# Landmark sums of two batches: strided sums on VectorE, or products with the identity on TensorE

## The chip, the cores and the metric

The kernel runs on one core of a Trainium2 chip. The metric is the device time of one execution in microseconds (us), as a median over runs. The engines are TensorE (PE, its weight loads PEld), VectorE (DVE), ScalarE (ACT), GpSimd (POOL) and SyncE (SP), whose queue issues most of the DMAs.

## What is computed

Three stages follow each other: attention by landmarks, a dense layer with squared ReLU, and a layer of eight experts of which each token uses one. Only the first matters here; its beginning is the sum over segments:

```python
batch, n_heads, seq, head_dim = (8, 8, 576, 64); m = 32; scale = 1.0 / np.sqrt(D)
q_lm = q.reshape(B, H, m, S // m, D).mean(axis=3)      # 32 landmarks, each the mean of 18 rows
k_lm = k.reshape(B, H, m, S // m, D).mean(axis=3)
A = sm(q, k_lm); Bm = sm(q_lm, k_lm); C = sm(q_lm, k)  # softmax of scaled scores
# Z: an iterated inverse of Bm, 6 steps
attn = A @ Z @ C @ v
h = np.maximum(x @ w_in, 0.0); x = (h * h) @ w_out     # x: attn, (4608, 512)
# then gate, argmax over 8 experts, that expert's two layers
```

Everything is fp32, up to the argmax.

## The kernel before

A batch's attention is a *unit*, written as a Python generator: the sums of keys and queries, transposes, landmarks, scores, softmax, the seven steps of the inverse, and a matrix `wt` by which `w_in` becomes G for this batch. The dense layer of a batch, `gemm`, takes G and the transposed A (`at`) and runs two column halves times 16 steps of `hp` (six products, L998), ReLU and square (ScalarE and VectorE, L1009 to L1012) and `acc` (twelve products, L1045). It is the main loop.

Batch 0's unit runs alone at first, in `prologue`, at a high priority, beside the conversion of the weights `w_in` and `w_out` (`convert`: two ScalarE operations, L153 and L154, two of VectorE, L163 and L164, one of GpSimd, L167, for each piece; `w_out` is split into two parts besides). Then come the first parts of G (`first_g_of`, L827, L834, L837), and `gemm(0)`, into which the unit of batch 1 is woven by a rate, and so on for each next batch. The program is traced once; a planner then lays down each engine's order by priority and readiness in its own model of the times. On the chip every engine takes its instructions in that fixed order.

A tile `t` holds the keys or the queries of four heads: 128 partitions (head, landmark) by 18 rows by 64 columns, loaded by one DMA of 576 KB from SP's queue. Keys and queries share three such buffers (one more for the last of batch 0). The next load is issued by `load_next` when a tile's transposes are done.

Batches 0 and 1 (`u["pe"]`, b below `PE_BATCHES`) turn keys and queries over by transposes on TensorE (`transposed`, L395, three to a bank, recorded under the helper's line L349, then a ScalarE copy L398). For the later batches VectorE does it.

The sums (`sums`) are the same for all batches: two strided VectorE reductions over the 18 rows (L382), and a GpSimd copy (L385) that puts the 64 columns a second time beside the first, since the scores need the landmarks in both halves of the partitions. `landmarks` transposes the sums of both head groups (two transposes) and copies the result out on ScalarE (L447). Products of the unit run through `matmul` and stand under L346.

PSUM banks come from `self.banks`: seven in the prologue, three in the first G, and from then on the three of `aux` alone, which the unit, G and the routing share.

Of the kernel before, what the change touches and what calls it, by code (L numbers as in the profile page):

```python
# [9 lines left out]
F32 = mybir.dt.float32  # L10
# [4 lines left out]
ALU = mybir.AluOpType  # L15
# [4 lines left out]
B, H, S, D = 8, 8, 576, 64  # L20
# [63 lines left out]
class Kernel:  # L84
# [214 lines left out]
    def constants(self):  # L299
        nc, cst, drm = self.nc, self.cst, self.drm  # L300
        self.ident = ident = cst.tile([128, 128], F32, name="ident")
        make_identity(nc, ident)
        self.win_d = {
            (n, k): drm.tile([128, 512], F32, name=f"win_{n}_{k}") for n in range(4) for k in range(KD)
        }
        self.at_d = [[drm.tile([128, S], F32, name=f"at_{b}_{g}") for g in range(2)] for b in range(B)]
        self.g_d = [[drm.tile([128, 2, 512], F32, name=f"g_{b}_{n}") for n in range(4)] for b in range(B)]
        self.x2_d = drm.tile([B, 128, KD, S], F32, name="x2_d")
        self.rt_d = drm.tile([B, 128, 2, NT], F32, name="rt_d")
        self.ls_d = drm.tile([B * NE, 2], I32, name="ls_d")  # L310

        self.rt = cst.tile([128, B, 2, NT], F32, name="rt")
        self.prim = cst.tile([32, B], I32, name="prim")
        self.flags = cst.tile([32, B, NE], F32, name="flags")

        self.hm = hm = cst.tile([128, 2, D], F32, name="hm")
        self.i32 = i32 = cst.tile([128, LM], F32, name="i32")
        self.h4 = h4 = cst.tile([128, 4], F32, name="h4")
        nc.vector.memset(hm, 0.0)
        nc.vector.memset(h4, 0.0)  # L320
        for h in range(4):
            p = slice(32 * h, 32 * h + 32)
            nc.vector.memset(hm[p, h % 2, :], 1.0)
            nc.vector.memset(h4[p, h:h + 1], 1.0)
            nc.vector.tensor_copy(out=i32[p, :], in_=ident[p, p])


        self.wg = cst.tile([128, KD, 32], F32, name="wg")
        nc.vector.memset(self.wg, 0.0)
        for j, w in enumerate((self.w_gate, self.w_og)):  # L330
            nc.gpsimd.dma_start(
                out=self.wg[:, :, NE * j:NE * (j + 1)], in_=w.rearrange("(k p) e -> p k e", p=128)
            )
        self.sel = cst.tile([128, 16], F32, name="sel")
        for h in range(4):
            p = slice(32 * h, 32 * h + 32)
            nc.vector.tensor_copy(out=self.sel[p, :], in_=ident[p, 32 * h:32 * h + 16])
        self.ones = cst.tile([128, 32], F32, name="ones")
        nc.vector.memset(self.ones, 1.0)
        self.desc = cst.tile([128, NE], F32, name="desc")  # L340
        for e in range(NE):
            nc.vector.memset(self.desc[:, e:e + 1], float(NE - e))
# [31 lines left out]

    def sums(self, u, nm, hg):

        if hg == 0:
            u[nm + "s"] = self.sm.tile([128, 2, 2, D], F32, tag=f"{nm}s", name="sums", bufs=1)
        s, t = u[nm + "s"][:, hg], self.qk[nm, u["b"], hg]
        for d in range(0, D, D // 2):  # L380
            ds = slice(d, d + D // 2)
            self.nc.vector.tensor_reduce(  # L382
                out=s[:, 0, ds], in_=t[:, :, ds].rearrange("p s d -> p d s"), axis=AX.X, op=ALU.add
            )
        self.nc.gpsimd.tensor_copy(out=s[:, 1], in_=s[:, 0])  # L385
# [53 lines left out]
    def landmarks(self, u, nm):  # L439
        nc = self.nc  # L440
        pd = self.bank()
        for hg in range(2):
            self.transpose(
                pd[:, 128 * hg:128 * hg + 128], u[nm + "s"][:, hg].rearrange("p c d -> p (c d)"), self.ident
            )
        lm = u[nm + "l"] = self.sm.tile([128, 2, 4, LM], F32, tag=f"{nm}l", name="lm", bufs=1)
        nc.scalar.copy(out=lm.rearrange("p g h l -> p (g h l)"), in_=pd[:, 0:256])  # L447
# [1026 lines left out]
```

## Time and profile before

| | |
|---|---|
| median of three runs | 1344.57 us (1343.83 to 1346.1) |
| profiled execution, its time | 1349.18 us |
| its span, first to last instruction | 1347.4 us |
| mean granted TensorE clock | 0.977 |
| TensorE busy | 1271.6 us, 94% |
| VectorE busy | 786.7 us, 58% |
| ScalarE busy | 628.3 us, 47% |
| GpSimd busy | 381.1 us, 28% |

Times in the rows are counted from the start of the span. A row of a timeline gives start, length, engine, line, operation, tiles, shapes and the number of instructions merged; in brackets how long the engine stood idle before it and what ended that.

### The profile page before, as it was taken

What the parts mean: (1) busy time and instruction counts of PE and PEld (TensorE: products, weight loads), DVE (VectorE), ACT (ScalarE), POOL (GpSimd) and SP (SyncE); (2) the same over time, 40 slices, a digit from 0 to 9 for tenths busy, and PEclk for the clock granted to TensorE, in tenths of its full rate; (3) what the DMA queues carried; (4) which work ended last, traced back from release to release, by engine and by line L of the source; (5) the groups of instructions that cost most, each with busy time, mean ns of one, the idle gap of its engine ahead of it and who ended that gap; (6) DMA issues with size and microseconds to landing.
All of it is one profiled execution on the core that took longest, in us unless ns stands there. A gap on an engine that the chain in (4) does not pass through costs nothing.

```text
span 1347.4 us, 25210 instructions
## 1 busy us (share of the span) xinstructions
PE 1271.6 (94%) x9458; PEld 1109.7 (82%) x9458; DVE 786.7 (58%) x1760; ACT 628.3 (47%) x1385; POOL 381.1 (28%) x305
## 2 busy tenths in 40 slices
PE   6577998999999999999999999999999999999995
PEld 3256867789688888898999999998898889888884
DVE  7999967668769898787643434454323323233231
ACT  5576464355544557545654334344334334334231
POOL 3556222113004035413622112024323313323110
PEclk8699998999999999999999999999999999999998
DMA  9855283472723337613652112024345345354231
GB/s 322 283 196 165 95 288 91 147 217 73 217 81 101 90 104 214 188 62 95 204 146 66 42 37 65 1 60 141 108 117 160 97 131 151 96 146 113 79 91 37
DMA packets 128574, 172.39 MB, mean 128 GB/s; under 512 B 12449, under 2 KB 85953, under 8 KB 128449
## 3 DMA queue, kind: packets, MB, share of 16 engines
q1 hardware_dynamic: 128352, 170.71, 42.2%
q8 instruction: 76, 1.25, 0.4%
q14 instruction: 50, 0.40, 0.1%
q0 software_dynamic: 96, 0.03, 0.0%
HBM read 128.19 MB, written 42.51 MB: 127 GB/s over the span
## 4 chain that ended last, share of the span: by engine, by line
PE 74%; DVE 14%; DMA 5%; issue 3%; ACT 2%; POOL 1%; SPq 0%; DVEq 0%; POOLq 0%; ACTq 0%
PE acc L1045 23%; PE hp L1231 15%; PE y L1257 13%; PE hp L998 11%; PE bank L346 6%; DVE sums L382 3%; DVE g L1010 2%; PE y L1268 2%; DVE gl L1012 2%; PE pl L1072 1%; DVE m L164 1%; DMA t<-in_q_dram 1%; DVE x L413 1%; DMA g<-gs 1%; DVE m L163 1%
## 5 line engine op out<-in xcount | busy, mean ns | idle before, releaser
L1045 PE MATMUL acc<-gh,wo 128*128 128x288 f32 x2048 | 456.9, 299 | 2.9 <-DVE wo L191 2.4
L1045 PEld LDWEIGHTS acc<-gh,wo 128*128 128x128 f32 x2048 | 342.8, 189 | 26.4 <-issue 16.0
L1045 PE MATMUL acc<-gl,wo 128*128 128x288 f32 x1024 | 288.2, 300 | 10.6 <-DVE gl L1012 10.1
L998 PE MATMUL hp<-ab,gb 128*128 128x288 f32 x1536 | 254.4, 300 | 0.8 <-DVE gb L837 0.5
L1010 DVE TENSOR_TENSOR g<-r 128x288 f32<-128x288 f32 x256 | 145.2, 568 | 160.5 <-ACT r L1009 159.7
L998 PEld LDWEIGHTS hp<-ab,gb 128*128 128x128 f32 x1536 | 218.0, 189 | 20.6 <-issue 6.9
L1009 ACT ACTIVATE r<-hp 128x288 f32<-128x288 f32 x256 | 105.4, 412 | 245.5 <-PE hp L998 240.9
L1231 PEld LDWEIGHTS hp<-xs,s 128*128 128x128 f32 x1536 | 210.7, 188 | 9.0 <-issue 0.9
L1231 PE MATMUL hp<-xs,s 128*128 128x288 f32 x1536 | 215.5, 295 | 0.0
L1045 PEld LDWEIGHTS acc<-gl,wo 128*128 128x128 f32 x1024 | 193.4, 189 | 23.3 <-DVE gl L1012 17.5
L1257 PE MATMUL y<-s,h 128*128 128x512 f32 x768 | 190.6, 395 | 0.0
L1257 PEld LDWEIGHTS y<-s,h 128*128 128x128 f32 x768 | 141.1, 188 | 29.5
L1012 DVE TENSOR_TENSOR gl<-g,gh 128x288 fp32r<-128x288 f32 x256 | 146.3, 572 | 25.8 <-ACT gh L1011 8.2
L191 POOL TENSOR_TENSOR s<-r,s 128x512 fp32r<-128x512 f32 x64 | 83.2, 1301 | 245.4 <-ACT s L188 225.1
L191 DVE TENSOR_TENSOR s<-r,s 128x512 fp32r<-128x512 f32 x64 | 50.3, 787 | 152.2 <-ACT s L188 152.1
L191 POOL TENSOR_TENSOR gb<-gr,gb 128x512 fp32r<-128x512 f32 x56 | 74.0, 1322 | 226.9 <-ACT gb L188 144.7
L188 ACT CAST s<-r 128x512 fp32r<-128x512 f32 x128 | 78.5, 616 | 117.0 <-PE y L1268 104.7
L1240 DVE SCALAR_TENSOR_TENSOR h<-hp,h 128x64 fp32r<-128x64 f32 (+2 forms) x192 | 62.7, 355 | 114.3 <-ACT h L1237 114.2
L1011 ACT ACTIVATE gh<-r 128x288 fp32r<-128x288 f32 x256 | 114.1, 446 | 6.5
L1237 ACT ACTIVATE h<-hp 128x288 fp32r<-128x288 f32 x128 | 52.6, 411 | 134.3 <-PE hp L1231 125.4
L382 DVE TENSOR_REDUCE sums<-t 128x32 f32<-128x576 f32 x64 | 71.1, 1164 | 12.6 <-DMA t<-in_q_dram 8.2
L191 POOL TENSOR_TENSOR xs<-xr,xs 128x1152 fp32r<-128x1152 f32 x16 | 45.8, 2864 | 68.3 <-ACT xs L188 63.2
(193 smaller groups left out, 1323.2 us busy)
## 6 DMA issues: line engine op xcount, KB each, us to landing
r<-in_moe_w_dram SPq DMA_DIRECT2D x128, 256.0 KB, 3.0
w<-win SPq DMA_DIRECT2D x80, 256.0 KB, 4.1
gr<-g SPq DMA_DIRECT2D x56, 256.0 KB, 3.2
t<-in_k_dram SPq DMA_DIRECT2D x16, 576.0 KB, 5.3
t<-in_q_dram SPq DMA_DIRECT2D x16, 576.0 KB, 4.8
v<-in_v_dram SPq DMA_DIRECT2D x48, 192.0 KB, 4.2
x_d<-x SPq DMA_DIRECT2D x16, 576.0 KB, 3.8
xr<-x_d SPq DMA_DIRECT2D x16, 576.0 KB, 4.5
```

Source lines behind the costliest of these rows:

```text
L188: hi = self.nc.scalar.copy(out=t[:, 0], in_=raw)
L191: (lo_eng or self.nc.gpsimd).tensor_tensor(out=t[:, 1], in0=raw, in1=t[:, 0].bitcast(F32), op=ALU.subtract)
L346: self.last_pe = self.nc.tensor.matmul(out, **kw)
L382: self.nc.vector.tensor_reduce(out=s[:, 0, ds], in_=t[:, :, ds].rearrange("p s d -> p d s"), axis=AX.X, op=ALU.add)
L998: mm = nc.tensor.matmul(hp[:, 0:HC], lhsT=g[:, l, hg, fs], rhs=at[:, r, hg, :], start=(i == 0), stop=(i == 5))
L1009: nc.scalar.activation(out=r, in_=hp[:, 0:HC], func=ACTF.Relu, scale=1.0 / 256)
L1010: nc.vector.tensor_tensor(out=g2, in0=r, in1=r, op=ALU.mult)
L1011: nc.scalar.activation(out=gh, in_=r, func=ACTF.Square)
L1012: nc.vector.tensor_tensor(out=gl, in0=g2, in1=gh.bitcast(F32), op=ALU.subtract)
L1045: nc.tensor.matmul(acc[m][:, 0:HC], lhsT=self.wo[f][:, l, ms], rhs=r, start=(f == 0 and i == 0), stop=(f == NFC - 1 and i == 2),)
L1231: nc.tensor.matmul(hp[:, 0:HC], lhsT=s1[:, l, kk, :], rhs=xs[j, c][:, r, kk, :], start=(k == 0), stop=(k == 3 * KD - 1),)
L1257: nc.tensor.matmul(acc[t], lhsT=l, rhs=s2[:, r, :], start=(first and k == 0), stop=(last and k == 2))
```

## The change

For batches 0 and 1 the sums are made by TensorE: nine products for each tile, each with two of the 18 rows as weights (128 rows by 2 x 64 columns) and the identity as the moving side, accumulated in one PSUM bank. The result is the sums already turned over, even and odd rows apart. ScalarE copies it out. `landmarks` then takes two products with a folding matrix (the identity's two halves added), which add even and odd rows and write the result to both halves of the partitions, in place of two transposes. The reductions and GpSimd's copies of these batches go. The other batches stay as they are.

```diff
+        self.fold = cst.tile([128, D], F32, name="fold")
+        nc.vector.tensor_tensor(out=self.fold, in0=ident[:, 0:D], in1=ident[:, D:], op=ALU.add)
...
     def sums(self, u, nm, hg):
+        if u["pe"]:
+            if hg == 0:
+                u[nm + "p"] = self.bank()
+                u[nm + "s"] = self.sm.tile([128, 2, 2, D], F32, tag=f"{nm}s", name="sums", bufs=1)
+            t, to = self.qk[nm, u["b"], hg], slice(128 * hg, 128 * hg + 128)
+            for r in range(9):
+                self.matmul(
+                    u[nm + "p"][:, to], lhsT=t[:, 2 * r:2 * r + 2].rearrange("p c d -> p (c d)"), rhs=self.ident,
+                    start=(r == 0), stop=(r == 8),
+                )
+            self.nc.scalar.copy(out=u[nm + "s"][:, hg].rearrange("p c d -> p (c d)"), in_=u[nm + "p"][:, to])
+            return
         if hg == 0:
...
     def landmarks(self, u, nm):
         nc = self.nc
         pd = self.bank()
-        for hg in range(2):
+        if u["pe"]:
+            for c in range(2):
+                self.matmul(
+                    pd[64 * c:64 * c + 64, 0:256], lhsT=self.fold, rhs=u[nm + "s"].rearrange("p g c d -> p (g c d)"),
+                    start=True, stop=True,
+                )
+        for hg in range(0 if u["pe"] else 2):
             self.transpose(
                 pd[:, 128 * hg:128 * hg + 128], u[nm + "s"][:, hg].rearrange("p c d -> p (c d)"), self.ident
             )
```

## Rows read from the trace of the kernel before

**Rows 1.** Totals of the page: busy time, share of the span, instructions.

```profile
PE 1271.6 (94%) x9458; PEld 1109.7 (82%) x9458; DVE 786.7 (58%) x1760; ACT 628.3 (47%) x1385; POOL 381.1 (28%) x305
```

**Rows 2.** Stretches of the span: length, busy time by engine, granted clock, DMA share, GB/s.

```profile
0.00:60.00 60.00, 33.17 (x356) 18.31 (x358) 52.29 (x121) 32.70 (x70) 25.42 (x30) 0.69 0.94 306
60.00:150.00 90.00, 72.41 (x595) 58.54 (x592) 88.61 (x152) 61.08 (x143) 48.51 (x37) 0.96 0.57 179
```

**Rows 3.** VectorE's timeline, 4 to 83 us.

```profile
4.64 8.47 DVE L382 TENSOR_REDUCE sums<-t 128x32 f32<-128x576 f32 x8 [0.68 <-DMA t<-in_k_dram]
...
20.39 0.81 DVE L497 TENSOR_REDUCE mc<-bank 128x1 f32<-128x288 f32 x2
...
36.38 2.19 DVE L382 TENSOR_REDUCE sums<-t 128x32 f32<-128x576 f32 x2
...
55.01 2.23 DVE L382 TENSOR_REDUCE sums<-t 128x32 f32<-128x576 f32 x2
...
60.24 0.41 DVE L837 TENSOR_TENSOR gb<-bank,gb 128x256 fp32r<-128x256 f32 x1
...
80.09 2.30 DVE L382 TENSOR_REDUCE sums<-t 128x32 f32<-128x576 f32 x2
```

**Rows 4.** TensorE's timeline, 4 to 60 us.

```profile
4.75 3.80 PE L349 MATMUL bank<-ident,t 128*128 128x128 f32 x18 [4.75 <-DMA t<-in_k_dram]
...
14.52 1.64 PE L346 MATMUL bank<-x,lm 64*32 64x288 f32 x11 [0.46 <-ACT lm L447]
...
16.68 1.97 PE L346 MATMUL bank<-x,lm 64*32 64x288 f32 x14
18.58 1.20 PE L349 MATMUL bank<-ident,t 128*128 128x128 f32 x9
...
38.83 0.86 PE L346 MATMUL bank<-eu 32*32 32x96 f32 x16 [2.50 <-DVE eu L633]
...
55.03 5.34 PE L827 MATMUL bank<-wf,wt 128*64 128x512 f32 x14 [0.55 <-ACT wt L660]
```

**Rows 5.** Stretches of one granted clock each, columns as in rows 2.

```profile
8.20:11.50 3.30, 0.93 (x6) 0.50 (x4) 3.30 (x4) 1.42 (x4) 0.47 (x2) 1.00 1.00 352
11.60:18.30 6.70, 4.36 (x50) 2.16 (x49) 5.71 (x8) 4.24 (x8) 2.91 (x3) 0.50 1.06 285
...
28.70:59.30 30.60, 16.96 (x180) 7.21 (x180) 27.76 (x49) 14.38 (x29) 16.88 (x14) 0.50 0.93 300
59.40:80.00 20.60, 16.46 (x93) 9.83 (x89) 19.72 (x35) 18.12 (x46) 9.79 (x8) 1.00 0.83 273
```

**Rows 6.** Products by shape (ns min/median/max, starts), and four in sequence.

```profile
L346 PEld LDWEIGHTS bank<-eu,dg x168: 186/191/192, 132.2 to 654.0; 128*128 128x128 f32 x168
L346 PE MATMUL bank<-eu,dg x168: 217/275/350, 132.2 to 654.0; 128*128 128x96 f32 x140, 128*128 128x64 f32 x28
...
L346 PE MATMUL bank<-w,wt x96: 592/592/644, 165.3 to 368.9; 128*64 128x512 f32 x96
...
132.19 0.66 PE L346 MATMUL bank<-eu,dg 128*128 128x96 f32 x4 [1.75 <-DVE dg L647]
```

**Rows 7.** ScalarE's copy of the landmarks, columns as in rows 6.

```profile
L447 ACT COPY lm<-bank x16: 367/373/379, 9.7 to 603.2; 128x256 f32<-128x256 f32 x16
```

**Rows 8.** TensorE's waits, 55 to 230 us: total us, times, longest.

```profile
PE bank L349 <- DVE gb L837: 2.9, 4, 1.2
```

**Rows 9.** SP's queue at 69 us; the page's issues (KB each, us to landing).

```profile
69.47 0.38 SPq L364 DMA_DIRECT2D t<-in_q_dram  x1
...
t<-in_q_dram SPq DMA_DIRECT2D x16, 576.0 KB, 4.8
```

**Rows 10.** The chain that ended last, TensorE's timeline and a stretch at 200 us.

```profile
195.14 9.89 DMA t<-in_q_dram
...
207.50 0.74 PE L346 MATMUL bank<-bc,dg 128*128 128x96 f32 x2 [4.38 <-DVE bc L587]
...
200.00:215.00 15.00, 9.95 (x98) 8.14 (x97) 6.91 (x16) 4.08 (x9) 3.54 (x4) 0.77 0.49 139
```

## Prediction

> **What bounds the kernel now.** I read four views, in this order. First the totals of the page and a table of stretches [rows 1, 2]: over the whole span TensorE is busy 94%, but not evenly. Up to 60 us it is busy 33.2 of 60 us, from 60 to 150 us 72.4 of 90 us, and after that (1271.6 - 33.2 - 72.4) = 1166.0 of 1197.4 us, 97%. VectorE is the mirror image: 88.6 of the 90 us between 60 and 150. So the head of the kernel hangs on VectorE and on the single chain of batch 0, and the rest, some 1,200 us, on TensorE. Time won in the head moves the rest forward; work added to TensorE costs its full length only after 150 us. The change touches batches 0 and 1 alone, whose landmark sums all lie before 83 us.
>
> Second, VectorE's timeline [rows 3]. A sum over one tile of 128 rows is two reductions of 1.1 us. Batch 0's eight stand back to back from 4.64 us, 8.47 us. Batch 1's eight come as four pairs, at 36.38, 55.01, 57.77 and 80.09 us: 2.19 + 2.23 + 2.23 + 2.30 = 8.95 us (the two pairs between 55 and 60 us are alike; one stands in the rows). The reader is to see where these fall: the pair at 36.38 stands in the midst of batch 0's inverse, and TensorE's next inverse product waits 2.50 us for VectorE's step of it [rows 4]; the two pairs at 55 to 60 us stand ahead of the low parts of G, which begin only at 60.24 us [rows 3], at the entry of the main loop, from where VectorE is never free again up to 150 us.
>
> Third, TensorE's timeline and its clock [rows 4, 5]. In the head TensorE is granted half speed from 11.6 to 18.3 and from 28.7 to 59.3 us. The 18 transposes from 4.75 us take 3.80 us, 0.21 us each, the nine at 18.58 us take 1.20 us, (1.20 - 0.28) / 8 = 0.12 us apart: the first are thus at half speed too, and the clock rose behind them.
>
> Fourth, the waits and the loads [rows 8, 9], used below.
>
> **The change, part by part.** Everything is summed against the profiled execution: span 1347.4 us, 1349.2 us with what lies around it. That is 4.6 us above the median of the runs, 1344.57; I carry the difference over to the median.
>
> *Removed.* Sixteen reductions, 8.47 us in batch 0 and 8.95 us in batch 1, and eight GpSimd copies, which count only as a link ahead of the landmarks: GpSimd is busy 25.4 and 48.5 us of the two stretches [rows 2].
>
> *Added on TensorE.* Four groups of nine products in each batch. The trace has no such product; the nearest are the fp32 products of the inverse with the same 128x128 weights. Seven batches times six steps times two halves make 84 products and there are 168 records [rows 6], so a product is two instructions. Four of them take 0.66 us, (0.66 - 0.28) / 3 = 0.13 us each; transposes of 128 columns give 0.12 us. One group of 18 instructions is thus 18 x 0.12 = 2.2 us at full clock and 18 x 0.21 = 3.8 us at half. Bounds: 18 x 0.10 = 1.9 us if the tail of the four is the longest record, 350 ns, and 18 x 0.19 = 3.4 us if each weight load stands open at its recorded 191 ns. I take 2.2 us, as the nearest rows run in sequence: 8.8 us a batch.
>
> *Added on ScalarE.* Eight copies of 128x128 out of PSUM. The 128x256 copy takes 0.37 us [rows 7]; I take 0.28 us each, between half of it and the whole.
>
> *Landmarks.* Two transposes of 0.12 us plus some 0.2 us of tail become two folding products over 256 columns, which write the two halves of the partitions. The nearest row is the 64-wide product of 512 columns, 592 ns for each of its records [rows 6]; 0.6 us instead of 0.4, so +0.2 us for each of four landmark sets. The tile for folding is one small VectorE operation ahead of 4.64 us, where VectorE stands idle 0.68 us waiting for the first load: nothing; without that cover some 0.2 us.
>
> *Where these fall: batch 0.* TensorE starts at 4.75 us. First group at half speed: to 8.6. Three groups and 18 transposes at full speed: 3 x 2.2 + 18 x 0.12 = 8.8 us, to 17.4. Copy, fold and landmark copy, 0.3 + 0.6 + 0.4: the first scores start at 18.7 instead of 14.52 us, 4.2 later. But TensorE, now busy without a break, should keep the full clock which it lost at 11.6 us, so the scores, 4.1 us to 18.65 before, take about half: 2 us back. And what follows the scores, VectorE's maxima, stands at 20.39 us, 1.7 us after them [rows 3], behind conversions of weights which will find VectorE free from 4.6 us on; of that another 1.2. Net +1.0 us, bounds 0 (all covered) and +4.2.
>
> *Batch 1, up to the main loop.* The pair at 36.38 goes: the inverse steps come 2.2 us earlier. The pairs at 55 to 60 go: VectorE takes conversions of weights in their place and enters its saturated stretch 4.46 us ahead. Against that, TensorE itself is busy with G's products from 55.03 us on, and the main loop follows right behind them. Batch 1's first sums need a PSUM bank, as its transposes do, which stand behind these products; so I place two groups there, ahead of the loop's first products: 2 x 2.2 = 4.4 us at full clock, 2 x 3.8 = 7.6 at half. VectorE goes on with conversions meanwhile, so part of this is idle time of TensorE taken up front: +2.6 us taken, bounds 0 and +7.6. Sum: -2.2 - 4.5 + 2.6 = -4.1.
>
> *Batch 1, in the main loop.* The pair at 80.09 goes, -2.3 us of a saturated VectorE. The other two groups, 4.4 us, lie beside 17.6 us of idle TensorE between 60 and 150 us [rows 2]: nothing. If that cover is gone, +4.4. The copies on ScalarE, 4 x 0.28, are +1.1 at most, and I take it whole, since ScalarE is busy 18.1 of 20.6 us from 59.4 us on [rows 5]; the folds, TensorE again, nothing.
>
> **Sum:** +1.0 - 4.1 - 2.3 + 1.1 = -4.3 us. Profiled: 1344.9; median 1340.3. A change of 0.2%, 2.7 us, is about what a measurement of this kernel can tell from none.
>
> One wait is new. Each of batch 1's sums is now in TensorE's queue, with the main loop behind it. The keys and queries come through three buffers; the last query tile is asked for at 69.47 us [rows 9], when the first key tile has been transposed, and a query tile lands 4.8 us after its issue in the median [rows 9]. VectorE took it up at 80.09, late enough never to wait. Also the query's bank is held from its first half to its second, one of the three that transposes, G and landmarks share; before, TensorE's transposes stood 2.9 us for such banks [rows 8].
>
> **Rivals.** *A: the new wait decides; slower.* The key groups push the transposes, and so that load, some 4 us back, to land at about 78 us, while the products stand in the queue where VectorE is no longer late. What such a wait costs is seen at 195 to 207 us: VectorE's sums wait for a load of queries, TensorE stands 4.38 us for what is queued behind them, and the clock falls, 0.77 over 200 to 215 us [rows 10]. Price: 4.4 us of standing and 15 x 0.23 = 3.4 us of lost clock against the -4.3, +3.5, and up to 4.4 for two groups that find no idle time, +7.9: 1348 to 1352.5. It decides once standing and lost clock pass 4.3 us. For it: the queue order is fixed beforehand. Against: TensorE has 17.6 us idle there.
>
> *B: no change.* Batch 0 is late by the full 4.2 us, or the groups fill TensorE's idle time while ScalarE takes over as the bound. -4.3 + 3.2 = -1: 1343.5. For it: from 59.4 to 80 us VectorE is busy 96%, ScalarE 88% and TensorE 80% [rows 5].
>
> *C: a larger gain.* All of VectorE's 8.95 us counts, batch 0 loses nothing, and the denser TensorE holds the full clock in the stretch 28.7 to 59.3 us. There the 14 products of G take 5.34 us [rows 4], 0.38 each; at full clock half, -2.7. -8.95 - 2.7 + 1.1 = -10.5: 1334. For it: the clock rose behind nothing but transposes. Against: the inverse leaves TensorE mostly idle there.
>
> A page speaks to C. The Trainium skill's "TensorE: Matmul & The Clock Gate", section "Part 4: PE-mode transpose", holds that transposes don't count as activity and don't engage the full clock; by it only products would lift the clock, and the new groups would do what the transposes couldn't, which by C's terms gives 1334. The trace disagrees: the 18 transposes from 4.75 us start 0.21 apart, nothing but transposes had run, and the clock was at full right behind them [rows 4, 5]. So C gets no more than its own evidence.
>
> **How the numbers follow.** Forecast (-8 to -2.7 us) 0.40, C 0.15, B 0.24, A 0.21. Faster by over 0.2%: 0.40 + 0.15 = 0.55; within: 0.24; slower: 0.21. The time is that of the forecast, 1340.3; alone it spans 1336.5 to 1342. The range leaves out what of C lies below 1333 us, some 0.07, and of A above 1349 us, some 0.12: 1333 to 1349.
>
> **What would show it.** Right: no reductions ahead of 100 us, 144 more TensorE records of 128 columns at 0.11 to 0.13 us each, scores of batch 0 starting between 17 and 19 us, the inverse's second product 2 us nearer to its first, VectorE less busy between 36 and 60 us, the main loop starting 1 to 4 us earlier, and a lead of about 4 us at 150 us. Wrong: the scores' delay still there at 34 us (batch 0's loss isn't recovered); TensorE idle with a wait for a query load or for a bank between 60 and 90 us (A); no lead at 150 us (B). Since all queues are ordered anew, a stall such as that of 203 us may also go, or come up elsewhere; that alone could move the time by 5 us either way.

## The result and the profile after

The changed kernel takes 1352.69 us (median of five runs, 1349.46 to 1354.41), the kernel before 1345.26 in the same comparison (1343.83 to 1346.1). The ratio is 1.0054, interval 1.0042 to 1.0066: slower by 0.54%, 7.3 us. The prediction, 1340.3 us and faster with a chance of 0.55, was wrong in sign; its range ended at 1349.

The totals of the page of the changed kernel stand against [rows 1]:

```profile
PE 1280.2 (95%) x9610; PEld 1122.4 (83%) x9610; DVE 775.2 (57%) x1745; ACT 630.8 (47%) x1393; POOL 377.9 (28%) x297
```

VectorE's busy time fell by 11.5 us, less than the 17.4 us of the sixteen reductions that went; TensorE's rose by 8.6, with 152 records more. The profiled spans, 1348.3 and 1347.4 us, are only 0.9 us apart: the profiled execution of before (1349.18) stood 3.9 us above the median of its runs, that of the changed kernel (1349.97) 2.7 us below the median of its own. The trace of before has a stall at 195 to 207 us [rows 10]; whether the timed runs have it no trace shows. So the comparison is made at a point ahead of that stall, the first product of the routing logits (tile pl, the end of the loop's first half): 163.7 us before, 170.5 after. That lateness of 6.8 us is the size of the timed loss.

A table of stretches of the changed kernel, against [rows 2]:

```profile
0.00:60.00 60.00, 32.97 (x418) 24.25 (x418) 41.93 (x110) 32.96 (x72) 24.55 (x25) 0.76 0.93 310
60.00:150.00 90.00, 75.46 (x628) 60.31 (x626) 80.21 (x130) 60.30 (x139) 44.89 (x34) 0.95 0.53 169
```

VectorE's busy time is 10.4 us less before 60 us and 8.4 less between 60 and 150, and the kernel is slower all the same. In the second stretch it is the ends that are emptier. In the middle of it VectorE is as full as before; the kernel before, then the changed one:

```profile
70.00:130.00 60.00, 46.95 (x429) 38.64 (x428) 59.55 (x98) 44.09 (x101) 35.88 (x27) 0.97 0.59 183
```

```profile
70.00:130.00 60.00, 46.77 (x350) 38.45 (x349) 59.45 (x88) 46.49 (x108) 39.38 (x29) 0.97 0.45 149
```

TensorE's timeline of the changed kernel, against [rows 4] (L348 is a product, L351 a transpose; the sums' products carry the tiles of transposes):

```profile
12.34 4.18 PE L348 MATMUL bank<-ident,t 128*128 128x128 f32 x36
16.45 1.08 PE L348 MATMUL bank<-sums,fold 128*64 128x256 f32 x8
...
18.12 0.43 PE L348 MATMUL bank<-x,lm 64*32 64x288 f32 x1
...
19.45 0.87 PE L351 MATMUL bank<-ident,t 128*128 128x128 f32 x6
23.98 0.55 PE L351 MATMUL bank<-ident,t 128*128 128x128 f32 x3 [3.65 <-ACT bc L553]
...
28.56 1.09 PE L351 MATMUL bank<-ident,ec 128*96 128x128 f32 x4 [2.96 <-ACT ec L529]
...
40.23 0.86 PE L348 MATMUL bank<-eu 32*32 32x96 f32 x16 [1.41 <-DVE eu L650]
...
51.96 0.86 PE L348 MATMUL bank<-eu 32*32 32x96 f32 x16 [4.54 <-DVE eu L658]
...
59.67 0.66 PE L351 MATMUL bank<-ident,wb 128*128 128x128 f32 x2 [4.14 <-DVE wb L661]
60.89 6.10 PE L852 MATMUL bank<-wf,wt 128*64 128x512 f32 x16 [0.55 <-ACT wt L685]
66.91 1.38 PE L348 MATMUL bank<-ident,t 128*128 128x128 f32 x10
68.05 1.04 PE L1023 MATMUL hp<-ab,gb 128*128 128x288 f32 x6
...
72.14 2.17 PE L348 MATMUL bank<-ident,t 128*128 128x128 f32 x18
```

From 4.86 to 17.5 us TensorE has no long break: nine products are 18 records (two groups take 4.18 us, one in the loop 2.17), the folds 8 records in 1.08, and the first scores start at 18.12 us, all near the forecast. But the 3.6 us by which they are late become 5.8 at the transposes of the exponentials (28.56 against 22.72), 5.9 at the first product of G (60.89 against 55.03) and 7.0 at the loop's first hp (68.05 against 61.03), where ten more records of batch 1's products stand just ahead.

Where the delay first grows is seen in ScalarE's timeline of the changed kernel (L153 and L154 convert a piece of weights, L553 and L529 are the softmax exponentials, L521 copies the scores out):

```profile
17.15 0.80 ACT L472 COPY lm<-bank 128x256 f32<-128x256 f32 x2 [0.33 <-PE bank L348]
22.16 0.66 ACT L153 ACTIVATE m<-raw 128x512 f32<-128x512 f32 x1 [4.21 <-DMA raw<-in_moe_w_in_dram]
22.73 0.66 ACT L154 ACTIVATE r<-raw 128x512 int32<-128x512 uint32 x1
23.28 0.28 ACT L553 ACTIVATE bc<-bank,mb 128x32 f32<-128x32 f32 x1
...
23.81 1.31 ACT L521 COPY ec<-bank 128x288 f32<-128x288 f32 x4
```

and in VectorE's, against [rows 3]:

```profile
12.12 0.43 DVE L163 TENSOR_SCALAR m<-m 128x512 int32<-128x512 int32 x1 [8.17 <-ACT m L153]
...
18.41 0.23 DVE L548 TENSOR_REDUCE mb<-bank 128x2 f32<-128x64 f32 x1 [0.67 <-PE bank L348]
...
22.86 0.43 DVE L163 TENSOR_SCALAR m<-m 128x512 int32<-128x512 int32 x1 [3.67 <-ACT m L153]
...
24.25 0.46 DVE L522 TENSOR_REDUCE mc<-bank 128x1 f32<-128x288 f32 x1
```

The reader is to see two things. The VectorE time that the change freed, 4 to 12 us, is idle: no weights have landed that it could convert. And when the scores are there, the queues hold a conversion that waits 4.21 us for its weights, with the softmax, the copies of the scores and VectorE's maxima behind it; these maxima come at 24.25 us, 20.39 before [rows 3].

### The profile page after: what moved, and what is told of

The parts are those of the page before. It is cut to its first block, busy times and chain, and to the rows that moved or that the text cites. A ratio compares the mean times of both kernels' runs of the same rounds, so it can differ in the third digit from the quotient of the medians.

```text
span 1348.3 us, 25495 instructions
## 1 busy us (share of the span) xinstructions
PE 1280.2 (95%) x9610; PEld 1122.4 (83%) x9610; DVE 775.2 (57%) x1745; ACT 630.8 (47%) x1393; POOL 377.9 (28%) x297
## 4 chain that ended last, share of the span: by engine, by line
PE 73%; DVE 13%; DMA 6%; issue 3%; ACT 2%; POOL 1%; SPq 1%; DVEq 0%; ACTq 0%; POOLq 0%
PE acc L1070 23%; PE hp L1256 15%; PE y L1282 13%; PE hp L1023 11%; PE bank L348 6%; PE y L1293 2%; DVE g L1035 2%; DMA raw<-in_moe_w_in_dram 2%; DVE gl L1037 2%; DVE sums L400 1%; DMA g<-gs 1%; PE pl L1097 1%; DVE m L163 1%; DVE x L431 1%; DVE m L164 1%
## 5 line engine op out<-in xcount | busy, mean ns | idle before, releaser
L1070 PEld LDWEIGHTS acc<-gh,wo 128*128 128x128 f32 x2048 | 341.7, 188 | 23.3 <-issue 17.4
L1035 DVE TENSOR_TENSOR g<-r 128x288 f32<-128x288 f32 x256 | 141.1, 552 | 161.9 <-ACT r L1034 161.0
L1037 DVE TENSOR_TENSOR gl<-g,gh 128x288 fp32r<-128x288 f32 x256 | 140.4, 549 | 25.2 <-ACT gh L1036 6.4
L400 DVE TENSOR_REDUCE sums<-t 128x32 f32<-128x576 f32 x48 | 53.8, 1171 | 9.2 <-DMA t<-in_q_dram 5.4
```

Of the source, the lines that this page charges most:

```text
L400: self.nc.vector.tensor_reduce(out=s[:, 0, ds], in_=t[:, :, ds].rearrange("p s d -> p d s"), axis=AX.X, op=ALU.add)
L1035: nc.vector.tensor_tensor(out=g2, in0=r, in1=r, op=ALU.mult)
L1037: nc.vector.tensor_tensor(out=gl, in0=g2, in1=gh.bitcast(F32), op=ALU.subtract)
L1070: nc.tensor.matmul(acc[m][:, 0:HC], lhsT=self.wo[f][:, l, ms], rhs=r, start=(f == 0 and i == 0), stop=(f == NFC - 1 and i == 2),)
```

## The experiments

One table of milestones from the timelines of the profiled executions (start in us of the first instruction of a kind on TensorE: scores of batch 0, transposes of its exponentials, the inverse, G, hp, logits), and the timed ratio to the kernel before:

| kernel | scores | ec | inverse | G | hp | logits | ratio (interval) |
|---|---|---|---|---|---|---|---|
| before | 14.52 | 22.72 | 34.35 | 55.03 | 61.03 | 163.7 | |
| the change | 18.12 | 28.56 | 40.23 | 60.89 | 68.05 | 170.5 | 1.0054 (1.0042, 1.0066) |
| e1 before again | 14.62 | 22.82 | 34.22 | 54.90 | 61.19 | 164.3 | 0.9998 (0.9985, 1.0011) |
| e2 batch 1 alone | 14.55 | 22.74 | 34.12 | 54.53 | 61.81 | 167.5 | 1.0049 (1.0036, 1.0061) |
| e3 batch 0 alone | 18.59 | 27.23 | 41.27 | 62.97 | 68.83 | 169.6 | 1.0055 (1.0042, 1.0068) |
| e4 conversion later | 18.53 | 27.23 | 40.95 | 62.07 | 69.10 | 171.8 | 1.0081 (1.0062, 1.0101) |
| e5 before, head late | 19.19 | 27.97 | 40.07 | 62.42 | 68.06 | 167.5 | 1.0029 (1.0017, 1.0042) |
| e6 one tile of batch 0 | 14.62 | 22.01 | 38.49 | 60.48 | 66.44 | 168.9 | 1.0030 (1.0017, 1.0042) |
| e7 e2, other pace | 14.67 | 22.87 | 34.43 | 54.85 | 61.91 | 168.1 | 1.0041 (1.0028, 1.0055) |
| e8 before, other pace | 14.63 | 22.84 | 34.55 | 55.23 | 61.90 | 163.7 | 0.9984 (0.9972, 0.9995) |
| e9 batch 1, 1 of 9 products | 14.74 | 22.93 | 33.31 | 53.73 | 59.68 | 163.5 | 1.0013 (1.0000, 1.0026) |
| e10 batch 1, products twice | 14.48 | 22.68 | 34.98 | 55.41 | 61.89 | 171.3 | 1.0055 (1.0039, 1.0072) |
| e11 both, 1 of 9 products | 13.14 | 21.17 | 35.06 | 54.74 | 59.90 | 159.8 | 0.9987 (0.9975, 0.9999) |
| e12 the change, other pace | 19.49 | 27.14 | 39.13 | 59.78 | 67.24 | 169.1 | 1.0054 (1.0034, 1.0073) |

The timed loss follows the lateness at the logits, within some 3 us for each kernel.

**The kernel before once more (e1).**

> The kernel before, unchanged, for a second trace of it. The profiled execution of before took 1349.2 us, its timed runs 1343.8 to 1346.1, so something of 3 to 5 us in that trace may not be typical; the stall at 195 to 207 us (a wait for a load of queries, 4.4 us of TensorE and half clock behind it) is the candidate. If so: time equal to before within 0.1%, a trace without that stall, or with a shorter one, and the first half of the main loop, whose end stood at 163.7 us, unchanged to 1 us. If the stall is typical, the second trace shows it too, at the same length.

It gave 1346.56 us against 1346.04, so the comparison tells no difference where there is none. Its profiled execution has the stall again, shorter (2.92 us of standing, 4.38 in [rows 10]):

```profile
206.83 0.74 PE L346 MATMUL bank<-bc,dg 128*128 128x96 f32 x2 [2.92 <-DVE bc L587]
```

**Each batch by itself (e2, e3).** In `sums` and `landmarks`, and in nothing else:

```diff
-        if u["pe"]:
+        if u["b"] == 1:      # e3: == 0
...
-        for hg in range(0 if u["pe"] else 2):
+        for hg in range(0 if u["b"] == 1 else 2):      # e3: == 0
```

> Batch 1's sums by products, batch 0's by reductions as before. Theory 'batch 0 pays' (the 5.9 us by which the first product of G is late, 60.89 instead of 55.03 us, are the whole loss, and batch 1's relief gives little): time 0 to -3 us against before, first scores at 14.5 us, first product of G at 52.5 to 55 us. Rival 'batch 1 pays' (its products stand in TensorE's queue with the main loop behind them, and VectorE's relief goes into conversions): +5 to +8 us, first half of the main loop longer than 102.7 us by that. Rival 'order' (each new order costs or gives some us anywhere): any sign, and the two parts don't add up.

> Batch 0's sums by products, batch 1's by reductions as before. 'Batch 0 pays': +6 to +10 us against before, first scores at 18.1 us, first product of G at 61 to 63 us, since batch 1's reductions are back in the inverse. 'Batch 1 pays': within 2 us of before, the 5.9 us at the first product of G made good later. 'Order': the sum of this and of batch 1 alone differs from the +7.4 us of the whole change by more than 3 us.

Batch 1 alone, from which the prediction had taken nearly all of its gain, loses 0.49%; batch 0 alone 0.55%; both together 0.54%. The losses don't add: with batch 0's already there, batch 1's products cost only 1.0 us more at the logits (169.56 to 170.52), without it 3.8. In e3 the loop's first half, hp to logits, takes 100.8 us instead of 102.7; a loop that starts late waits less, and batch 1's products then take up what it has won. That last sentence is argued from the milestones, not tested.

**Is it the one conversion in ScalarE's queue (e4)?** The fourth conversion is ordered behind batch 0's copies of the scores and the first exponentials (a second edit, left out here, keeps the program from reaching that conversion before these are placed):

```diff
+            elif i == 3:
+                for a in self.hold:          # batch 0's ec copies and bc exponentials
+                    self.follow(first, a)
+                    self.follow(second, a)
```

> The changed kernel, but the fourth conversion of weights stands behind batch 0's score copies and first softmax on ScalarE, not ahead of them; ahead of them it waited 4.21 us for its load, with batch 0's softmax ready behind it. Theory 'batch 0 pays' with that wait as a part: softmax of batch 0 at about 19.5 instead of 23.28 us, first product of G 2 to 4 us earlier (57 to 59 us), time 2 to 4 us below the changed kernel (+3.5 to +5.5 against before). If the loads of weights bound the head anyway: first product of G still at 60 to 61 us and time as the changed kernel.

It moved those copies ahead: they stand at 19.94 us, and the transposes of the exponentials start at 27.23 instead of 28.56. But the first product of G came later, 62.07, and the time is 1.0081. The conversion itself runs right behind the copies, at 21.11 us, 1 us sooner than in the changed kernel. From the exponentials' transposes to G this kernel takes 34.8 us, the changed one 32.3; what takes the 2.5 us was not followed. So that one wait, plain as it is in the timeline, is not a cause whose removal gives the time back.

**A late head without any product (e5).** The kernel before, with three more reductions in front of batch 0's last sums:

```diff
-        for d in range(0, D, D // 2):
+        again = 3 if u["b"] == 0 and nm == "q" and hg == 1 else 0
+        for d in [0] * again + [0, D // 2]:
```

> The kernel before, with three of batch 0's reductions done a second time (same output), 3 x 1.13 = 3.4 us more of VectorE ahead of the first scores and no product anywhere. A test of the chain of batch 0 alone. Theory 'batch 0's chain sets the start of the main loop and a delay there is kept': first scores 3.4 us later (18.0 us), first product of G 3 to 4.5 us later (58 to 59.5), time +2.5 to +5 us. Rival 'the loads of weights set the start': first product of G within 1 us of 55, time within 1.5 us of before. Rival 'order': first product of G and time move by something unrelated to 3.4 us.

The scores start 4.7 us late; it is 5.3 at the exponentials' transposes, 5.7 at the inverse and 7.4 at the first product of G. TensorE's timeline of this kernel:

```profile
19.19 1.65 PE L346 MATMUL bank<-x,lm 64*32 64x288 f32 x11 [0.67 <-ACT lm L448]
...
27.97 1.10 PE L349 MATMUL bank<-ident,ec 128*96 128x128 f32 x6 [2.27 <-ACT ec L505]
```

No product makes sums there, so a delay of batch 0's scores grows without the products too. It grows at another place, though: in the changed kernel 2.2 us before the exponentials' transposes and nothing from there to G, here 0.6 and 2.1. One size of delay was tried. The time rose by 0.29%, 3.9 us, which is what is left of 7.4 us at the end of the first half (3.8).

**One tile by products (e6).** Only the last query tile of batch 0 is summed on TensorE, the other three on VectorE, to take the reductions' tail off the path (beside the change):

```diff
+        if u["b"] == 0 and nm == "q" and hg == 1:
+            ps, t = self.bank(), self.qk[nm, u["b"], hg]
...
+                    ps[:, 0:128], lhsT=t[:, 2 * r:2 * r + 2].rearrange("p c d -> p (c d)"), rhs=self.ident,
...
-        for hg in range(0 if u["pe"] else 2):
+        for hg in range(1 if last else 2):
```

> The kernel before, but the last of batch 0's four tiles (the second of the queries) is summed by nine products while VectorE sums the other three; its half of the landmarks comes by the folding products, the other half by the transpose as before. Both engines then work side by side: VectorE is done at about 11 us, TensorE's nine products of 2.2 us end at about 12, first scores at 12.5 to 13.5 instead of 14.52 us. If batch 0's chain is what counts: first product of G 1 to 2 us earlier, time 1 to 2.5 us below before. If not, or if ScalarE's conversions stand ahead of the copies: time within 1.5 us of before, or above it.

The scores started no earlier (14.62), the exponentials' transposes 0.7 us earlier, and then nearly 5 us were lost on the way to the inverse (16.5 us from there, 11.6 before). TensorE's timeline of this kernel shows where:

```profile
22.01 1.09 PE L351 MATMUL bank<-ident,ec 128*96 128x128 f32 x4 [2.71 <-ACT ec L526]
...
28.30 1.19 PE L348 MATMUL bank<-x,lm 64*32 64x288 f32 x8
...
30.53 1.18 PE L348 MATMUL bank<-x,lm 64*32 64x288 f32 x8 [0.45 <-ACT x L413]
31.64 0.65 PE L348 MATMUL bank<-v,et 96*32 96x64 f32 x14
```

Sixteen records of score products, eight before, were laid between the transposes and the third group of products with `et`; that group starts at 31.64, 9.6 us behind the first of the transposes, against 5.2 before (22.72 to 27.88). TensorE was granted half speed from 20.3 us on there, before it had full speed from 18.4 to 28.6. A small edit thus laid the queues anew and cost 0.30%; how much of it is the order and how much the clock was not separated.

**The pace of the conversions (e7, e8, e12).** One constant decides how often a conversion may go between loop steps:

```diff
-CONV_TICKS = 5
+CONV_TICKS = 2
```

> Batch 1's sums by products as in the run of batch 1 alone (+0.49%), with the conversions of weights paced at half of the program's steps instead of four fifths. In that run the last conversion came at 121.9 instead of 133.8 us, while the seventh step of the main loop came at 92.9 instead of 85.0: theory 'VectorE's relief goes into conversions, the loop's steps wait behind products and conversions'. By it the main loop's first half (102.7 us before, 105.7 there) shrinks to 100 to 103 and the time to -2 to +3 us against before. Rival 'the products themselves, 8 us of TensorE in front of the loop's steps, are the loss': the half stays at 105 or more, the time at +5 to +8.

> The kernel before with the same slower pace of conversions, as the control of the run beside it. If the pace alone helps or harms, it shows here: expected -2 to +4 us, since VectorE is full between 61 and 150 us and the second parts of the dense layer need the conversions in time. What counts is the difference between the two runs: under +2 us if the products' loss was the relief gone into conversions, +5 us or more if it is the products' own time on TensorE.

> The change with CONV_TICKS 2 instead of 5, the pacing that took 1.6 us from the kernel before (e8). If conversions that ride on VectorE's relief delayed batch 0: first product of G nearer 55 than 61 us and 1347 us. If the pace acts only behind the first loop step, as in e7: 1351 us, within 2 us of the change itself.

In e2's kernel it hardly moved the conversions (the last at 122.2 instead of 121.9 us), so that run says nothing of conversions in the loop's way. What the three say together: another order of the same work moves the time by 0.08% (1.0049 to 1.0041), 0.16% and 0.00%. The loss of the change is three times the largest of these; but e6 shows that a small edit of the kernel can move more, 0.30%. The kernel before with this pace is the one version here with the whole computation that beats both kernels, 1345.21 against 1346.83 us, and only just.

**How much do the products cost, how much is VectorE's relief worth (e9, e10, e11)?** These decide. The nine products are done once, twice, or only the first of them is done, and nothing else is edited (e9 and e11 leave out eight of nine parts of the sums, so what they compute is not the layer):

```diff
-            for r in range(9):
+            for r in range(1):                        # e9 (batch 1 alone), e11 (both batches)
+            for r in [*range(9), *range(9)]:          # e10 (batch 1 alone)
```

> Products in batch 1 alone, as in e2, but one of the nine of each of the four blocks is left out of no more than its first: eight of nine are left out, so batch 1's sums hold one block row instead of nine. TensorE's work for them falls from 4 x 2.0 to 4 x 0.22 us, 7.3 us less; what VectorE is spared stays. If the products' own time on TensorE, ahead of the loop steps, is what batch 1 loses: e2's 5.7 us loss becomes a gain of about 1.5 us, 1345 us, and the loop's first half ends near 160.5. If the loss comes from the order alone (VectorE's freed time goes to conversions, the steps queue otherwise): within 1.5 us of e2, 1352 us, first half near 167.5.

> Products in batch 1 alone, each block's nine done twice (the second start overwrites the first, so the sums stay right): 8.2 us more on TensorE, nothing else changed. If the products' own time is the loss: 1352 + 8 = 1360 us, first half at about 175.5. If the order alone is: within 1.5 us of e2, 1352 us. Half of it, 1356 us, if TensorE's idle time between 61 and 150 us takes half.

> The change with one product of nine in each block of both batches (sums hold one block row instead of nine). In the head TensorE then has 4 x 0.2 instead of 4 x 2.0 us beside its 18 transposes, so the first scores start at about 12 us, before VectorE's reductions ended (14.5). If the head's loss is the products in series on TensorE: the first inverse product starts by 34 us, the first product of G by 54 us, the first half ends at 160 us or earlier, the time is 1340 to 1343 us. If the landing and conversion of the weights set the head and the freed VectorE time is worth nothing: first product of G at 54.5 to 56 us in spite of scores 2 us earlier, time 1344 to 1346 us.

For batch 1 the logits start at 163.5, 167.5 and 171.3 us with one of nine products, nine and eighteen. TensorE's added work between these is 4 x 16 and 4 x 18 records of 0.12 us, 7.7 and 8.6 us, and 4.0 and 3.8 us of it are paid: about half in both steps. That is a rough size: it is read from one execution of each, and the granted clock between 60 and 150 us differs, 0.92, 0.91 and 0.96. The products in e10, ahead of and between the loop's steps (compare 72.14 above):

```profile
68.86 4.29 PE L348 MATMUL bank<-ident,t 128*128 128x128 f32 x36 [0.69 <-ACT sums L393]
73.07 1.08 PE L852 MATMUL bank<-wf,wt 128*64 128x512 f32 x4
74.08 1.06 PE L1023 MATMUL hp<-ab,gb 128*128 128x288 f32 x6
```

The timed ratios show the first of these steps, 1.0013 to 1.0049, more clearly than the second, 1.0049 to 1.0055 (the medians rise by 2.3 us); the dose is read from the milestones.

And e9 tells what the other side is worth. It is without batch 1's eight reductions (8.95 us) and with nearly no products, and it is not faster than before: 163.5 against 163.7 us at the logits, 1.0013 in time. The copies, the folds and the hold on the shared PSUM banks stay, so this is not VectorE's relief alone; and the granted clock from 60 to 150 us is 0.92, against 0.96 before, a rival that no run sets aside. The lead that there is gets lost on the way: the first six steps of the loop start 1.4 to 2.5 us sooner than before, the seventh at 89.15 us, 4.1 later, and from there they run now ahead, now behind. TensorE in e9, between the sixth step and the seventh:

```profile
85.38 1.12 PE L348 MATMUL bank<-sums,fold 128*64 128x256 f32 x4 [2.86 <-DVE gb L862]
...
89.15 0.96 PE L1023 MATMUL hp<-ab,gb 128*128 128x288 f32 x6
```

It waits for VectorE's low part of G, ahead of which VectorE's row has a conversion (L163 and L164, from 82.35 us to 84.5).

The stretch from 60 to 150 us of e9, then e10, columns as in [rows 2]:

```profile
60.00:150.00 90.00, 73.64 (x598) 61.08 (x597) 83.51 (x141) 60.49 (x143) 45.04 (x34) 0.92 0.51 168
```

```profile
60.00:150.00 90.00, 77.92 (x676) 66.56 (x673) 76.50 (x126) 58.68 (x134) 45.11 (x33) 0.96 0.54 168
```

Before, VectorE was busy 88.61 us there and the time was the same as e9's; in e10 it is busy 76.50 and the kernel is slower by 0.55%. VectorE's busy time and the kernel's time have come apart.

Nor is VectorE's busy time the same thing as its work. Up to the logits it is busy 146.7 us in e9 and 151.8 before, 5.1 us less, not 8.95, with the eight reductions gone and as many other operations as before, but for the one that makes the folding matrix. The same 32 conversions (L163 and L164) take 55.5 us of it in e9, 51.6 before, and 61.2 in the changed kernel. The second of their operations up to 165 us, total us and mean ns, before and in the changed kernel:

```profile
L164 DVE SCALAR_TENSOR_TENSOR m<-raw,m 128x512 int32<-128x512 int32 x32 | 26.6, 832 | 0.4
```

```profile
L164 DVE SCALAR_TENSOR_TENSOR m<-raw,m 128x512 int32<-128x512 int32 x32 | 32.7, 1023 | 0.8
```

One such operation takes 0.67 to 1.66 us before and 0.65 to 1.92 after. What stretches it was not tested; the freed time went in part into this.

The upper bound of the whole idea is e11, both batches with nearly no products. TensorE and VectorE in the head of e11:

```profile
11.54 0.65 PE L348 MATMUL bank<-sums,fold 128*64 128x256 f32 x4 [0.35 <-ACT sums L393]
...
21.17 1.08 PE L351 MATMUL bank<-ident,ec 128*96 128x128 f32 x4 [4.41 <-ACT ec L529]
```

```profile
12.20 0.43 DVE L163 TENSOR_SCALAR m<-m 128x512 int32<-128x512 int32 x1 [8.24 <-ACT m L153]
```

The scores start 1.4 us before those of the kernel before, and the first product of G 0.3 us before (54.74): this lead is not handed on to G, whereas the delays grew. But the loop's first half takes 99.9 us, 102.7 before and 103.8 in e9, and the logits start 3.9 us sooner than before. From e9 to e11, with batch 0's reductions gone as well, it is 3.7 us at the logits and 0.26% in time (1.0013 to 0.9987, the intervals just apart). So batch 0's relief is worth some 3.5 us in this pair, gained in the loop and not in the head; how is not traced. The whole kernel gains 0.13%, 1.8 us, with an interval that nearly reaches 1. From e11 to the change the eight products of nine that were left out cost 1.0054 - 0.9987 = 0.67%, 9.0 us of 8 x 16 x 0.12 = 15.4 us of TensorE.

## Why the prediction was wrong, step by step

- *The price of a group, 2.2 us, the folds and copies.* Right: 2.17 us for one group and 4.18 for two at full clock, 0.27 us for a copy; the four folds of a batch, 8 records, took 1.08 us in batch 0.
- *First scores at 18.7 us.* Right, 18.12. The full clock held from 7.8 to 24.9 us, as forecast (the granted clock reads 1.00 already from 4.0 to 7.7 us here and from 4.70 to 8.10 before, where records start 0.21 us apart; that TensorE began at half speed is read from this spacing alone), and 2 us or more were won back on TensorE itself: the transposes behind the scores start at 19.45 us, against 18.58 before [rows 4], so 3.6 us had become 0.9.
- *"Net +1.0" for batch 0.* This step failed. It let the conversions use VectorE's free time from 4.6 us on and so take 1.2 us off the path. VectorE stood idle 8.17 us for want of weights, a conversion came between scores and softmax, and batch 0 was 5.9 us late at the first product of G. With 15.1 us of reductions gone before 60 us, the 15th conversion starts on ScalarE only 2.2 us sooner (57.1 us, 59.3 before). DMA is busy 0.93 of the head after, 0.94 before; that the stream of weights sets the pace there fits this and was not tested. By e5 a delay of 4.7 us at the scores grows to 7.4; by e11 against e9 batch 0's 8.47 us on VectorE are worth nothing at the first product of G (54.74 and 53.73 us) and 3.7 at the logits.
- *"-2.2 - 4.5" and "-2.3" for batch 1's pairs.* This is the larger failure: e9, which lacks all four pairs and nearly all products, is 0.2 us ahead at the logits. Each term went its own way. The -2.2 came and was lost again: the second product of the inverse starts 1.90 us behind the first, 4.48 before, but two later waits grew, ahead of the fifth product to 4.54 us (51.96 above; 2.29 before) and for `wb` to 4.14 us (59.67 above). From the inverse's first product to G's it is 20.7 us in both. The wait for `wb` before:

```profile
53.82 0.66 PE L349 MATMUL bank<-ident,wb 128*128 128x128 f32 x2 [2.55 <-DVE wb L636]
```

  In the changed kernel VectorE makes `wb` behind a long conversion:

```profile
57.27 1.92 DVE L164 SCALAR_TENSOR_TENSOR m<-raw,m 128x512 int32<-128x512 int32 x1
59.11 0.41 DVE L661 TENSOR_TENSOR wb<-eu,hm 128x256 f32<-128x256 f32 x1
```

  The -4.5 had the path wrong. In e9 the low parts of G begin 3.8 us sooner (56.44 us, 60.24 before), but the loop's first hp follows the first product of G by 5.95 us, 6.00 before: sixteen records of G's products on TensorE, 5.77 us in both, fill that time, and not VectorE. Of the -2.3 nothing is seen: e9's lead, 2.5 us at the loop's sixth step, was gone by the seventh. The prediction read VectorE's 88.6 of 90 us as a bound that time taken off would lower. Its row held conversions of weights that were not urgent (the last at 133.8 us before, at 121.6 in e9) between operations that TensorE waits for, and the order put conversions into the freed time. TensorE's waits from 61 to 164 us for the low half of the squared ReLU (gl) stayed: 4.8 us before, 4.9 in e9.
- *"+2.6" for TensorE and "nothing" for the groups in the loop.* Too small, by some 1.4 us. About half of the products' time is paid, some 4 us of batch 1's 8.6, though TensorE stood idle 17.6 of those 90 us. That idle time lies between steps whose order is fixed, and a group of 2 us goes in front of a step as a block (72.14 above).
- *Copies +1.1.* Not measured alone.
- *Rival A.* Its sign was right, its new wait was not the cause, and its second price, up to 4.4 us for groups that find no idle time, is near the 4 us that batch 1's products cost. The last query load is issued 9 us later than before [rows 9]. SP's queue in the changed kernel:

```profile
78.37 0.38 SPq L366 DMA_DIRECT2D t<-in_q_dram  x1
```

  But TensorE's waits from 60 to 110 us (total us, times, longest) name no load of queries, and only 1.8 us in which products of the unit stand for VectorE's part of G:

```profile
PE acc L1070 <- DVE gl L1037: 3.3, 3, 2.5
PE bank L348 <- DVE gb L862: 1.8, 2, 1.4
```

- *Rival B.* Batch 0 was late by more than its 4.2 us (5.9 at the first product of G) and the groups were not free; it had still counted VectorE's gains, and so came out at no change.
- *Rival C.* The clock of the inverse's stretch rose little, and its gain is not seen. Two stretches after, the head and the inverse's one of [rows 5]:

```profile
7.80:24.90 17.10, 12.74 (x144) 11.00 (x144) 8.06 (x14) 10.10 (x27) 4.61 (x4) 1.00 1.04 338
28.70:59.30 30.60, 16.12 (x258) 9.55 (x258) 26.67 (x53) 17.31 (x35) 16.33 (x13) 0.61 0.90 297
```

  Half speed, 1.2 GHz, still holds for most of the second (0.61), while the inverse leaves TensorE idle. The rule of the Trainium skill's "TensorE: Matmul & The Clock Gate", section "Part 4: PE-mode transpose", by which products would engage the clock where transposes don't, is not decided by this run: products and transposes alternate in the head after. In the kernel before, the transposes alone went from 421 ns a record at 5 us to 273 ns at 8.3, which speaks against it.

What stays open: what VectorE's relief of batch 1 would be worth without the copies, folds, held banks and the lower clock of e9; what stretches VectorE's conversions; why e11's loop is shorter than e9's; why e4's kernel loses more; why earliness at the scores is lost again in e11 (the inverse starts 0.7 us later than before, with the exponentials' transposes 1.6 us earlier), and how e6's 5 us divide between order and clock.

## What to carry to other kernels

An engine at 98% is a bound only as far as its work is due: ask which instructions of its row are waited for, and what the order will put into time that is freed. Here it put conversions with slack there, some of them in front of work that was waited for, and 8.95 us of reductions taken off (batch 1) were worth nothing, 17.4 us (both batches) 1.8. Work that is moved to an engine with idle time is not free when that time lies between steps of a fixed order; test it with the work left out and with it doubled before it is tuned. In a head where a chain of small steps shares in-order queues with work that waits for DMA, a delay can grow on its way (3.6 to 5.9 us, 4.7 to 7.4), and a lead need not be handed on (1.4 to 0.3).

## What was not expected of the hardware

A product of 128x128 fp32 weights with 128 columns costs, as two records, 2 x 0.11 to 0.12 us in sequence, twice a transpose of the same size; the weight loads, 186 to 192 ns each in the record, are hidden in it. One VectorE operation of one shape (L164, 128x512) took 0.65 to 1.92 us. And a profiled execution can lie off the median of the timed ones to either side: 1349.18 against 1345.26 and 1352.49 against 1346.56 us for the kernel before, with a stall between 203 and 207 us in both, 1349.97 against 1352.69 for the changed one; a difference of a few microseconds between two profiled spans was here no measure of the change.
